# Linear attention, RMS norm and two MLPs on one core: q times kv in one float32 product, one function for the inverse root, and another model of time behind the order

## The chip, the cores and the metric

The kernel runs on one core of a Trainium2 chip. The time is the device time of one execution in microseconds (us). Runs of the kernel before gave 1581.61, 1582.32 and 1583.42 us; their median, 1582.32, is the time that the change is measured against. The engines of the core are named as in the profile: PE (TensorE, matmuls; PEld is its weight load), DVE (VectorE), ACT (ScalarE), POOL (GpSimd) and SP (SyncE, which here only issues DMAs). Each works through its own list of instructions in order.

## What is computed

Eight batches of eight heads with 576 rows of 64 go through linear attention without a softmax, each row is divided by its root mean square, and the result passes two MLPs whose weights are 512 x 2048 and 2048 x 512.

```python
kv = np.einsum('bhsd,bhse->bhde', k, v)
out = np.einsum('bhsd,bhde->bhse', q, kv)
rms = np.sqrt(np.mean(out * out, axis=-1, keepdims=True) + 1e-06)
x = (out / rms * g_norm)            # then heads side by side: x is 4608 x 512

h = x @ w_in                        # first MLP
g = np.where(h >= 1, h, np.where(h <= -1, 0.0, (h + 1) ** 2 / 4))
x = g @ w_out

h = x @ w_in2                       # second MLP
r = np.maximum(h, 0.0)
return (r * r) @ w_out2
```

## The kernel before

All inputs are float32. Nearly every product is made of three matmuls in a rounded 32-bit format: each operand is split into a high part (a cast, on ACT) and a remainder (a subtract, on DVE), and high x high, high x remainder and remainder x high are summed in one bank. `mm3` and `mm_group` issue such threes; in the profile they are L242 and L880. Tiles hold features across the 128 partitions and 512 of a batch's 576 rows along the free axis; the 64 rows that are left of each batch are gathered and go through at the end.

The work has two parts.

In the **blocks** (to about 540 us) the batches 0 to 4 of the first MLP run one after the other, 16 steps each. A step multiplies x by one 128-wide piece of w_in (`h_stage`, banks ph), forms u with two passes of ACT and one of DVE (L704, L228, L706), splits it (`g_stage`: cast L221 and subtract L234 into gs), and two steps later adds its product with w_out into four banks acc (`out_stage`). At the end of a block the four acc banks are evicted (ev) and stored to DRAM as x1d. Beside these steps stand: the attention of the next batch, the loads and splits of the weights (raw, d, j, w, s, wt), and their stores back to DRAM (wsd), from which the second part takes its weights as ws. Those stores are issued by ACT (`owe` and `pay`) or by SP.

In the **phases** (from about 523 us) two batches are multiplied together by a scheme with seven products in place of eight. Phase n has an input half (banks ph{n}, 336 matmuls) and an output half (banks po{n}, 336 matmuls); n runs from 0 to 6, and 6 is the narrow one with the rows left over. The attention of batches 5 to 7 is hosted inside phases 0 and 1.

The **attention** of a batch b goes over four pairs of heads hp, in this chain. `kv_stage` (L486 on PE, bank pkv) multiplies k and v of a pair, or of two pairs at once, and copies the two 64 x 64 blocks of each pair out of the bank, into kvbd, one of two tiles with zeros off its blocks: high part by an ACT cast (L221), remainder by DVE (L499). `t_stage` transposes q on DVE (L565) and splits it: cast by ACT (L221, qT0), remainder by DVE (L567, qT1). `o_stage`, once for each half of 288 rows, multiplies (three matmuls at L242, bank po), squares the bank twice on ACT (L588 rounded, L589 exact), scales it by g (L213) and, after the second half, takes the remainder of the squares on DVE (L594). `r_stage` sums the squares of each half over the head with a matrix of ones (L608, bank pr), takes the logarithm of each half (L609), one exponential over both halves (L611), squares that (L228), makes a Newton step for the inverse root with the banks pr (L526, L622 or L529) and multiplies by the scaled product. Its result is split into x (batches 1 to 4: L221, L234), or stored to DRAM (batches 5 to 7). The first two pairs of batch 1 (`WHOLE`) are not split: their q times kv is one float32 matmul for each half (L576). Batch 0 has its own short forms (`o_first`, `r_first`), all in float32. pkv, po and pr share the banks of one small pool, so a kv product of a later pair can be behind a pr whose bank has not been read out.

The **order** of all this is set in two layers. The code lists the stages by slots (`attention` and the hooks), and a scheduler then orders the instructions of every engine by priority and by a model of when each would be ready. An engine follows its list strictly. DMAs of SP and ACT take, in the scheduled order, one of eight lanes in turn, and a DMA starts its issue when the one that had the lane before it has landed; while ACT waits to issue a store, its further instructions wait too.

Of the kernel before, what the change touches and what calls it, by code (L numbers as in the profile page):

```python
# [16 lines left out]

LN_SCALE = 2.0**-44  # L20
LN2 = 0.6931471805599453


# [54 lines left out]
def linear_attention_rms_two_mlps(  # L78
# [115 lines left out]
    lnb = const.tile([P, 1], F32, name="lnb")  # L194
    expb = const.tile([P, 1], F32, name="expb")
# [3 lines left out]
    kvbd = [const.tile([P, 2, P], F32R, name=f"kvbd{i}") for i in range(2)]  # L199
# [274 lines left out]
    def kv_stage(*pairs):  # L474
# [12 lines left out]
        for n, (b, hp) in enumerate(pairs):  # L487
            for j in range(2):
                s = slice(j * D, (j + 1) * D)
                d = slice(n * P + j * D, n * P + (j + 1) * D)  # L490
                if b == 0:
                    copy(engine("kv_hi", b), kv0[s, hp, s], ps[s, d])
                    continue
                if (b, hp) in WHOLE:
                    copy(engine("kv_hi", b), kvw[s, hp % 2, s], ps[s, d])
                    continue
                t = kvbd[turn[b, hp] % len(kvbd)]
                copy(engine("kv_hi", b), t[s, 0, s], ps[s, d])
                nc.vector.tensor_tensor(t[s, 1, s], ps[s, d], t[s, 0, s].bitcast(F32), ALU.subtract)  # L499
# [34 lines left out]
    def r_first(hp):  # L534
# [3 lines left out]
        for half in range(2):  # L538
# [3 lines left out]
            nc.scalar.activation(y[:, half], m, AF.Ln, bias=lnb, scale=LN_SCALE)  # L542
# [13 lines left out]
    def t_stage(b, hp):  # L556
        work = [ap1.tile([P, S], F32, tag=f"wk{n}", name=f"wk{n}_{b}_{hp}") for n in range(2)]
        if (b, hp) in WHOLE:
            qT = ap1.tile([P, S], F32, tag="hl0", name=f"qT_{b}_{hp}")
            nc.vector.transpose(qT, qs.pop((b, hp)))  # L560
            hl[b, hp] = (work, qT)
            return
        qT = ap1.tile([P, S], F32, tag="wk2", name=f"qf_{b}_{hp}")
        parts = [ap1.tile([P, S], F32R, tag=f"hl{n}", name=f"qT{n}_{b}_{hp}") for n in range(2)]
        nc.vector.transpose(qT, qs.pop((b, hp)))  # L565
        copy(engine("q_hi", b), parts[0], qT)
        engine("q_lo", b).tensor_tensor(parts[1], qT, parts[0].bitcast(F32), ALU.subtract)  # L567
        hl[b, hp] = (work, parts)

    def o_stage(b, hp, half):  # L570
        work, parts = hl[b, hp]
        kv = kvbd[turn[b, hp] % len(kvbd)]
        c = slice(half * U, (half + 1) * U)
        if (b, hp) in WHOLE:
            ps = bank(b, f"po_{b}_{hp}_{half}")
            nc.tensor.matmul(  # L576
                ps[:, :U], kvw[:, hp % 2, :], parts[:, c], start=True, stop=True
            )
# [7 lines left out]
        ps = bank(b, f"po_{b}_{hp}_{half}")  # L586
        mm3(ps[:, :U], lambda a: kv[:, a, :], lambda a: parts[a][:, c], True, True)
# [8 lines left out]
    def r_stage(b, hp):  # L596
# [6 lines left out]
        for half in range(2):  # L603
# [5 lines left out]
            nc.scalar.activation(y[:, c], m, AF.Ln, bias=lnb, scale=LN_SCALE)  # L609
            ms.append((c, m))  # L610
        nc.scalar.activation(y, y, AF.Exp, bias=expb, scale=-0.5)  # L611
        pool, tag = (ap1, "wk2") if b < PLAIN else (ap2, "q")
        t = pool.tile([P, S], F32, tag=tag, name=f"t_{b}_{hp}")
        square(engine("y", b), t, y)
        for c, m in ms:
            newton(t[:, c], m)
        if b < PLAIN:
            norm(t, y, o)
# [3 lines left out]
        nc.vector.scalar_tensor_tensor(t, t, -3.0, y, op0=ALU.add, op1=ALU.mult)  # L622
        nc.vector.tensor_tensor(o, o, t, ALU.mult)
# [548 lines left out]
    nc.scalar.preload_act_table_set("natural_log_exp_and_others")  # L1172
# [18 lines left out]
    for t in kvbd:  # L1191
        nc.vector.memset(t.bitcast(F32), 0.0)
# [4 lines left out]
    nc.vector.memset(lnb, LN_SCALE * 1e-6)  # L1197
    nc.vector.memset(expb, -22.0 * LN2)
# [131 lines left out]
```

## Time and profile before

| | before |
|---|---|
| runs, median of 3 | 1582.32 us |
| profiled execution, its own time | 1577.18 us |
| its span in the profile | 1575.4 us |
| PE busy, 7633 matmul records | 1544.0 us (98%) |
| PE weight loads | 1268.9 us (81%) |
| DVE busy | 1195.8 us (76%) |
| ACT busy | 929.3 us (59%) |
| DMA | 388 MB, mean 246 GB/s |

How to read it: busy times are sums over the whole span, so they are averages over stages with different limits. Matmuls are pipelined and overlap in their records; a PE that is busy can still be slowed by what it is fed. The stage windows among the rows below have these columns: the window in us, its length, busy time with the count of instructions for PE, PEld, DVE, ACT and POOL, then the granted clock of PE as a share of 2.4 GHz, the share of the time in which the DMA engines were busy, and GB/s. The profiled execution took 1.78 us more than its span, and 5.14 us less than the median of the runs.

### The profile page before, as it was taken

The page shows a single profiled execution, that of the slowest core. Times are in us where ns is not written, and L with a number is a line of the kernel's source. Part 1 is how long each engine was busy: PE and PEld are TensorE (multiplying, and loading weights), DVE is VectorE, ACT ScalarE, POOL GpSimd, SP SyncE. Part 2 cuts the span into 40 slices and gives each one's busy share as a digit, 9 for nine tenths or more (in the row PEclk, how much of TensorE's full clock was granted, in tenths as well). Part 3 has the DMA queues.
Part 4 walks back from the last instruction along what each step waited for, and adds up shares of the span by engine and source line. Part 5 has one row for each costly group of instructions (what it writes and reads, how often), then busy time and mean ns, then how long its engine had stood idle before and what let it go on. Part 6 is the DMA issues. An engine that isn't in the chain of part 4 may idle for free.

```text
span 1575.4 us, 22379 instructions
## 1 busy us (share of the span) xinstructions
PE 1544.0 (98%) x7633; PEld 1268.9 (81%) x7633; DVE 1195.8 (76%) x2112; ACT 929.3 (59%) x1751; POOL 13.4 (1%) x30
## 2 busy tenths in 40 slices
PE   9999989999999999999989999999999999999999
PEld 5787768878877788787778888888888888888899
DVE  6975878786989678975689788868974597559666
ACT  5976666766756566735576466546653464446354
POOL 0000000000000000000000000000000000000000
PEclk9999999999999999999999999999999999999999
DMA  9676899796899966878767877776776676977797
GB/s 286 199 246 193 286 307 327 229 292 208 256 353 346 320 195 207 261 219 226 229 199 234 226 242 242 225 220 196 243 232 208 198 243 199 243 236 221 224 387 254
DMA packets 330914, 388.17 MB, mean 246 GB/s; under 512 B 197808, under 2 KB 223408, under 8 KB 330800
## 3 DMA queue, kind: packets, MB, share of 16 engines
q1 hardware_dynamic: 299904, 330.63, 69.2%
q10 hardware_dynamic: 30896, 56.11, 9.5%
q8 instruction: 61, 1.00, 0.3%
q14 instruction: 53, 0.43, 0.1%
HBM read 300.42 MB, written 86.25 MB: 245 GB/s over the span
## 4 chain that ended last, share of the span: by engine, by line
PE 84%; DVE 6%; ACT 5%; DMA 3%; issue 1%; SPq 0%; ACTq 0%; DVEq 0%
PE ph L880 32%; PE po L880 29%; PE acc L242 10%; PE ph L242 9%; PE pkv L486 1%; PE po L242 1%; PE pr L608 1%; DMA wsd<-s 1%; DVE s L189 1%; DVE u L706 1%; PE pwarm L1183 1%; DMA ws<-wsd 1%; DMA rest<-in_v_dram 0%; DVE t L809 0%; DMA wt<-wsd 0%
## 5 line engine op out<-in xcount | busy, mean ns | idle before, releaser
L880 PE MATMUL ph<-x,ws 128*128 128x512 f32 (+1 forms) x2352 | 507.1, 376 | 0.5 <-DVE e L936 0.5
L880 PEld LDWEIGHTS ph<-x,ws 128*128 128x128 f32 x2352 | 419.4, 189 | 79.5 <-DVE e L936 1.2
L880 PE MATMUL po<-t,ws 128*128 128x512 f32 x2016 | 461.7, 390 | 1.5 <-DMA ws<-wsd 0.8
L880 PEld LDWEIGHTS po<-t,ws 128*128 128x128 f32 x2016 | 377.1, 188 | 82.0 <-DVE t L809 3.3
L809 DVE TENSOR_TENSOR t<-g,t 128x512 fp32r<-128x512 f32 (+1 forms) x336 | 215.6, 647 | 84.1 <-ACT t L221 81.7
L221 ACT CAST t<-g 128x512 fp32r<-128x512 f32 (+1 forms) x336 | 195.5, 591 | 120.7 <-PE po L880 62.9
L242 PE MATMUL ph<-x,w 128*128 128x512 f32 x960 | 243.1, 396 | 7.6 <-DVE u L706 6.0
L242 PEld LDWEIGHTS ph<-x,w 128*128 128x128 f32 x960 | 177.4, 189 | 50.5 <-DVE u L706 10.5
L242 PE MATMUL acc<-gs,w 128*128 128x512 f32 x528 | 134.4, 398 | 3.5 <-DVE u L706 1.5
L957 ACT ACTIVATE g<-h 128x512 f32<-128x512 f32 (+1 forms) x120 | 70.4, 589 | 95.8 <-DVE h L946 95.8
L242 PEld LDWEIGHTS acc<-gs,w 128*128 128x128 f32 x528 | 98.6, 190 | 25.6 <-DVE u L706 2.0
L946 DVE CUSTOM_DVE_ANT_0 h<-ph,e 128x512 f32<-128x512 f32 (+1 forms) x120 | 76.1, 636 | 51.6 <-PE ph L880 47.6
L936 DVE TENSOR_TENSOR e<-ph,e 128x512 f32<-128x512 f32 (+1 forms) x112 | 72.1, 649 | 56.2 <-PE ph L880 47.8
L242 PE MATMUL acc<-gs,wt 128*128 128x512 f32 x432 | 106.5, 394 | 1.9 <-DVE gs L234 1.9
L242 PEld LDWEIGHTS acc<-gs,wt 128*128 128x128 f32 x432 | 81.8, 190 | 19.2 <-DVE gs L234 2.4
L221 ACT CAST x<-xr 128x512 fp32r<-128x512 f32 (+1 forms) x98 | 57.1, 590 | 41.7 <-DVE xr L860 23.5
L221 ACT CAST gs<-u 128x512 fp32r<-128x512 f32 x80 | 49.7, 622 | 47.4 <-DVE u L706 39.1
L706 DVE SCALAR_TENSOR_TENSOR u<-u,ph 128x512 f32<-128x512 f32 x80 | 54.4, 680 | 30.0 <-ACT u L228 29.9
L704 ACT ACTIVATE u<-ph,halfb 128x512 f32<-128x512 f32 x80 | 55.3, 691 | 24.7 <-PE ph L242 18.8
L234 DVE TENSOR_TENSOR gs<-u,gs 128x512 fp32r<-128x512 f32 x80 | 54.8, 686 | 17.1 <-ACT gs L221 16.6
L933 ACT COPY e<-ph 128x512 f32<-128x512 f32 (+1 forms) x56 | 30.8, 553 | 58.4 <-PE ph L880 51.5
L809 DVE TENSOR_TENSOR x<-xr,x 128x512 fp32r<-128x512 f32 (+1 forms) x98 | 62.6, 644 | 2.0 <-ACT x L221 1.9
(135 smaller groups left out, 1620.9 us busy)
## 6 DMA issues: line engine op xcount, KB each, us to landing
ws<-wsd SPq DMA_DIRECT2D x392, 512.0 KB, 4.4
wsd<-s ACTq DMA_DIRECT2D x96, 512.0 KB, 5.7
wt<-wsd SPq DMA_DIRECT2D x36, 512.0 KB, 5.5
raw<-in_moe_w_in_dram SPq DMA_DIRECT2D x32, 512.0 KB, 7.0
raw<-in_moe_w_out_dram SPq DMA_DIRECT2D x32, 512.0 KB, 6.1
xr<-x1d SPq DMA_DIRECT2D x36, 256.0 KB, 5.2
out_dram<-ov SPq DMA_DIRECT2D x142, 64.0 KB, 3.7
wsd<-w SPq DMA_DIRECT2D x17, 512.0 KB, 4.0
```

The lines of the kernel that those rows point to most:

```text
L189: lo.tensor_tensor(t[:, :, 1, :], src, t[:, :, 0, :].bitcast(F32), ALU.subtract)
L221: return e.copy(dst, src)
L234: lo = engine(op + "_lo", phase).tensor_tensor(t[:, 1, :], src, t[:, 0, :].bitcast(F32), ALU.subtract)
L242: nc.tensor.matmul(dst, wt(a), xt(c), start=first and n == 0, stop=last and n == 2)
L704: nc.scalar.activation(u, ps, AF.Relu, bias=halfb, scale=0.5)
L706: nc.vector.scalar_tensor_tensor(u, u, 1.0, ps, op0=ALU.min, op1=ALU.max)
L809: engine2(op + "_lo").tensor_tensor(t[:, 1, :], src, t[:, 0, :].bitcast(F32), ALU.subtract)
L880: nc.tensor.matmul(ps, wt(a), xt(c), start=first and n == 0 and i == 0, stop=last and n == len(lhs) - 1 and i == 2, skip_group_check=True,)
L933: nc.scalar.copy(e[i, 1], bank)
L936: nc.vector.tensor_tensor(e[i, p], bank, e[i, 1], ALU.add)
L946: nc.vector._custom_dve(TENSOR_ADD_SAT, out=h, in0=bank, in1=add, s0=float("inf"), s1=0.0)
L957: nc.scalar.activation(g, h, AF.Square)
```

## The change

Three things change. The context that schedules the program is given the option `schedule_with_timeline_sim=True`, so that the scheduler uses a finer model of time for each instruction. q times kv is one float32 matmul for each half in all batches from 1 on, so qT is not split, kvbd holds one float32 block matrix, and the four steps that made the parts go (26 casts and 26 subtracts for q, 52 subtracts for kv, and 104 matmuls). And the inverse root is one function of ACT for each half, `Abs_reciprocal_sqrt` with the bias 1e-6, in place of the logarithm for each half and the exponential over both; the scaled product o is multiplied by the root's estimate y beside the square, and the Newton step then ends in one operation. 32 activations go; DVE has as many operations there as before, in another order.

```diff
-    kvbd = [const.tile([P, 2, P], F32R, name=f"kvbd{i}") for i in range(2)]
+    kvbd = [const.tile([P, P], F32, name=f"kvbd{i}") for i in range(2)]
...
-                t = kvbd[turn[b, hp] % len(kvbd)]
-                copy(engine("kv_hi", b), t[s, 0, s], ps[s, d])
-                nc.vector.tensor_tensor(t[s, 1, s], ps[s, d], t[s, 0, s].bitcast(F32), ALU.subtract)
+                copy(engine("kv_hi", b), kvbd[turn[b, hp] % len(kvbd)][s, s], ps[s, d])
...
-    def norm(t, y, o):
-        nc.vector.scalar_tensor_tensor(t, t, -3.0, y, op0=ALU.add, op1=ALU.mult)
-        nc.vector.tensor_tensor(t, o, t, ALU.mult)
+    def norm(dst, t, o):
+        nc.vector.scalar_tensor_tensor(dst, t, -3.0, o, op0=ALU.add, op1=ALU.mult)
...
         if (b, hp) in WHOLE:
...
-        qT = ap1.tile([P, S], F32, tag="wk2", name=f"qf_{b}_{hp}")
-        parts = [ap1.tile([P, S], F32R, tag=f"hl{n}", name=f"qT{n}_{b}_{hp}") for n in range(2)]
+        qT = ap1.tile([P, S], F32, tag="hl0", name=f"qT_{b}_{hp}")
         nc.vector.transpose(qT, qs.pop((b, hp)))
-        copy(engine("q_hi", b), parts[0], qT)
-        engine("q_lo", b).tensor_tensor(parts[1], qT, parts[0].bitcast(F32), ALU.subtract)
-        hl[b, hp] = (work, parts)
+        hl[b, hp] = (work, qT)
...
+        ps = bank(b, f"po_{b}_{hp}_{half}")
+        nc.tensor.matmul(ps[:, :U], kv, qT[:, c], start=True, stop=True)
...
-        ps = bank(b, f"po_{b}_{hp}_{half}")
-        mm3(ps[:, :U], lambda a: kv[:, a, :], lambda a: parts[a][:, c], True, True)
...
-            nc.scalar.activation(y[:, c], m, AF.Ln, bias=lnb, scale=LN_SCALE)
+            nc.scalar.activation(y[:, c], m, AF.Abs_reciprocal_sqrt, bias=epsb)
             ms.append((c, m))
-        nc.scalar.activation(y, y, AF.Exp, bias=expb, scale=-0.5)
         pool, tag = (ap1, "wk2") if b < PLAIN else (ap2, "q")
         t = pool.tile([P, S], F32, tag=tag, name=f"t_{b}_{hp}")
         square(engine("y", b), t, y)
+        nc.vector.tensor_tensor(o, o, y, ALU.mult)
         for c, m in ms:
             newton(t[:, c], m)
         if b < PLAIN:
-            norm(t, y, o)
+            norm(t, t, o)
...
-        nc.vector.scalar_tensor_tensor(t, t, -3.0, y, op0=ALU.add, op1=ALU.mult)
-        nc.vector.tensor_tensor(o, o, t, ALU.mult)
+        norm(o, t, o)
...
-    nc.scalar.preload_act_table_set("natural_log_exp_and_others")
+    nc.scalar.preload_act_table_set("abs_reciprocal_sqrt_and_small")
...
-    nc.vector.memset(lnb, LN_SCALE * 1e-6)
-    nc.vector.memset(expb, -22.0 * LN2)
+    nc.vector.memset(epsb, 1e-6)
...
-    with _tile.TileContext(nc) as tc:
+    with _tile.TileContext(nc, schedule_with_timeline_sim=True) as tc:
```


The option moves instructions on all engines. Three places show how; in the names, ph1 and po1 are phase 1, pkv_7_0 is the kv product of pair 0 of batch 7, and the numbers at the ends count tiles. A suffix xN means N matmuls in a row.

On PE in phase 1, between the last pr of batch 6 and the first q times kv of batch 7, before:

```order
L608 MATMUL pr_6_3_0_7611<-s2_6_3_7503,ones_123 128x288
L608 MATMUL pr_6_3_0_7611<-s2lo_6_3_7540,ones_123 128x288
L880 MATMUL ph1_5_2_7513<-x2_1_3_0_6723,ws2_0_1_3_7455 128x512 x3
L880 MATMUL ph1_5_2_7513<-x2_1_3_1_6925,ws2_0_1_3_7455 128x512 x3
L880 MATMUL ph1_5_3_7523<-x2_1_3_0_6723,ws2_0_1_3_7455 128x512 x3
L880 MATMUL ph1_5_3_7523<-x2_1_3_1_6925,ws2_0_1_3_7455 128x512 x3
L608 MATMUL pr_6_3_1_7615<-s2_6_3_7503,ones_123 128x288
L608 MATMUL pr_6_3_1_7615<-s2lo_6_3_7540,ones_123 128x288
L242 MATMUL po_7_0_0_7710<-qT0_7_0_7631,kvbd0_131 128x288
```

After, with rows left out in the middle that are all of phase 1:

```order
L586 MATMUL pr_6_3_1_7362<-s2_6_3_7260,ones_123 128x288
L586 MATMUL pr_6_3_1_7362<-s2lo_6_3_7291,ones_123 128x288
L857 MATMUL ph1_6_5_7423<-x2_1_6_1_6650,ws2_0_2_6_7264 128x512
L857 MATMUL ph1_1_4_7386<-x2_1_2_0_6469,ws2_0_2_2_7293 128x512 x3
L857 MATMUL ph1_1_4_7386<-x2_1_2_1_6673,ws2_0_2_2_7293 128x512 x3
...
L857 MATMUL ph1_6_5_7423<-x2_1_7_0_6399,ws2_0_2_7_7338 128x512 x3
L857 MATMUL ph1_6_5_7423<-x2_1_7_1_6621,ws2_0_2_7_7338 128x512 x2
L557 MATMUL po_7_0_0_7451<-qT_7_0_7376,kvbd0_130 128x288
```

The product po_7_0_0, which stood directly behind pr_6_3_1, has moved behind 29 matmuls of phase 1, and is one matmul.

On PE a little later in phase 1, at the sums of squares of pair (7,1), before, with the two pr halves back to back:

```order
L608 MATMUL pr_7_1_0_7998<-s2_7_1_7893,ones_123 128x288
L608 MATMUL pr_7_1_0_7998<-s2lo_7_1_7928,ones_123 128x288
L608 MATMUL pr_7_1_1_8002<-s2_7_1_7893,ones_123 128x288
L608 MATMUL pr_7_1_1_8002<-s2lo_7_1_7928,ones_123 128x288
L880 MATMUL ph1_5_6_7978<-x2_1_5_0_6593,ws2_0_3_5_7851 128x512 x3
```

After, with rows of phase 1 left out:

```order
L586 MATMUL pr_7_1_0_7723<-s2_7_1_7628,ones_123 128x288
L586 MATMUL pr_7_1_0_7723<-s2lo_7_1_7657,ones_123 128x288
L857 MATMUL ph1_6_6_7609<-x2_1_4_0_6520,ws2_0_3_4_7607 128x512 x3
L857 MATMUL ph1_6_6_7609<-x2_1_4_1_6720,ws2_0_3_4_7607 128x512 x3
...
L857 MATMUL ph1_5_6_7703<-x2_1_3_1_6697,ws2_0_3_3_7632 128x512 x3
L586 MATMUL pr_7_1_1_7727<-s2_7_1_7628,ones_123 128x288
L586 MATMUL pr_7_1_1_7727<-s2lo_7_1_7657,ones_123 128x288
```

Between the two halves, whose banks come from the pool that pkv and po use too, 18 matmuls of phase 1 now stand.

On PE at the end of block 0, from the last pr of batch 1 to the first matmul on the x made from it (x1_1_3), before, with rows of blocks 0 and 1 left out:

```order
L608 MATMUL pr_1_3_1_1418<-s2_1_3_1323,ones_123 128x288
L608 MATMUL pr_1_3_1_1418<-s2lo_1_3_1354,ones_123 128x288
L242 MATMUL ph1_0_14_1432<-x1_0_2_221,w1_0_14_1087 128x512
L242 MATMUL ph1_0_14_1432<-x1_0_3_222,w1_0_14_1087 128x512 x3
...
L242 MATMUL acc1_0_0_850<-gs1_0_14_1450,w1_1_14_1302 128x512 x3
L242 MATMUL acc1_0_1_851<-gs1_0_14_1450,w1_1_14_1302 128x512 x3
L242 MATMUL ph1_1_0_1502<-x1_1_3_705,w1_0_0_302 128x512
```

After, without a gap:

```order
L586 MATMUL pr_1_3_0_1385<-s2lo_1_3_1325,ones_123 128x288
L586 MATMUL pr_1_3_1_1389<-s2lo_1_3_1325,ones_123 128x288
L234 MATMUL acc1_0_1_844<-gs1_0_15_1457,w1_1_15_1348 128x512 x3
L234 MATMUL acc1_0_2_845<-gs1_0_15_1457,w1_1_15_1348 128x512 x3
L234 MATMUL acc1_0_3_846<-gs1_0_15_1457,w1_1_15_1348 128x512 x3
L478 MATMUL pkv_2_0_1490<-v_2_0_1330,k_2_0_1327 64x64 x8
L478 MATMUL pkv_2_0_1490<-rest0_128 64x64 x2
L478 MATMUL pkv_2_0_1490<-v_2_1_1336,k_2_1_1333 64x64 x8
L234 MATMUL ph1_1_0_1472<-x1_1_3_699,w1_0_0_300 128x512
```

The first matmul on x1_1_3 stood 43 matmuls behind pr_1_3_1, and now stands behind nine of acc1_0 and a kv product of batch 2: the x that is read is made in a chain over ACT and DVE from that pr.

## Rows read from the trace of the kernel before

**Rows 1.** Stage windows; columns as named under the table of the profile above.

```profile
0.00:52.00 52.00, 48.60 (x277) 30.88 (x277) 38.92 (x88) 35.04 (x68) 3.67 (x14) 1.00 0.95 278
52.00:540.00 488.00, 474.91 (x2363) 382.38 (x2362) 386.86 (x724) 330.16 (x643) 9.69 (x16) 0.99 0.84 273
540.00:881.60 341.60, 330.30 (x1635) 270.84 (x1636) 264.88 (x441) 202.92 (x397) 0.00 (x0) 0.99 0.76 225
881.60:1491.20 609.60, 609.60 (x2690) 504.40 (x2690) 450.15 (x722) 319.55 (x536) 0.00 (x0) 1.00 0.74 224
```

**Rows 2.** Chain of waits, late links: start us, length us, what.

```profile
881.59 76.16 PE ph L880 x336
...
1531.47 40.33 PE po L880 x336
```

**Rows 3.** PE's waits in 52:540, then 540:882: total us, times, longest.

```profile
PE ph L242 <- DVE u L706: 6.0, 7, 2.5
...
PE po L242 <- ACT qT L221: 3.9, 1, 3.9
PE pr L608 <- DVE kvbd L499: 3.5, 1, 3.5
PE pr L608 <- ACT wk L213: 1.9, 2, 1.3
```

**Rows 4.** A window as in rows 1, and a link of the chain.

```profile
718.60:724.00 5.40, 5.40 (x21) 4.49 (x21) 3.49 (x7) 3.79 (x7) 0.00 (x0) 0.68 1.03 250
...
718.90 4.32 PE ph L880 x12
```

**Rows 5.** Instruction groups by form: busy us, mean ns | idle us before.

```profile
L609 ACT ACTIVATE wk<-pr,lnb 128x288 f32<-128x288 f32 x56 | 26.8, 504 | 15.7 <-PE pr L608 15.5
L526 DVE SCALAR_TENSOR_TENSOR t<-pr,t 128x288 f32<-128x288 f32 x64 | 26.6, 450 | 3.4 <-ACT t L228 3.2
...
L611 ACT ACTIVATE wk<-wk,expb 128x576 f32<-128x576 f32 x28 | 22.0, 784 | 0.3
...
L588 ACT ACTIVATE s<-po 128x288 fp32r<-128x288 f32 x52 | 21.6, 415 | 27.1 <-PE po L242 23.8 <-DVE d L274 2.9 <-issue 0.3
...
L567 DVE TENSOR_TENSOR qT<-qf,qT 128x576 fp32r<-128x576 f32 x26 | 19.6, 753 | 5.8 <-ACT qT L221 5.5
...
L228 ACT ACTIVATE t<-wk 128x576 f32<-128x576 f32 x28 | 19.2, 685 | 0.2
...
L221 ACT CAST qT<-qf 128x576 fp32r<-128x576 f32 x26 | 17.4, 669 | 7.9 <-DVE qf L565 7.6
...
L221 ACT CAST x<-t 128x512 fp32r<-128x512 f32 x20 | 12.3, 617 | 16.2 <-DVE t L530 16.1
...
L499 DVE TENSOR_TENSOR kvbd<-pkv,kvbd 64x64 fp32r<-64x64 f32 x52 | 11.4, 220 | 9.9 <-ACT kvbd L221 9.1
```

**Rows 6.** Chain links of a float32 and a split pair, then their groups.

```profile
65.33 0.97 PE po L576 x4
...
780.24 0.79 PE po L242 x6
...
L242 PE MATMUL po<-qT,kvbd 128*128 128x288 f32 x156 | 29.8, 304 | 5.3 <-ACT qT L221 4.1 <-DVE qT L567 1.1
...
L576 PE MATMUL po<-qT,kvw 128*128 128x288 f32 x8 | 2.3, 411 | 0.0
```

**Rows 7.** Timeline near 750: start, length, instruction, [idle before <- releaser].

```profile
751.04 0.66 ACT L221 CAST qT<-qf 128x576 fp32r<-128x576 f32 x1
...
751.80 0.67 PE L242 MATMUL po<-qT,kvbd 128*128 128x288 f32 x2 [3.89 <-ACT qT L221]
```

**Rows 8.** Timelines near 228 and 498, ACT and PE.

```profile
228.09 0.63 ACT L228 ACTIVATE u<-u 128x512 f32<-128x512 f32 x1 [4.83 <-DMA rest<-in_v_dram]
...
229.49 4.55 PE L242 MATMUL ph<-x,w 128*128 128x512 f32 x12 [2.50 <-DVE u L706]
...
498.52 0.69 ACT L704 ACTIVATE u<-ph,halfb 128x512 f32<-128x512 f32 x1 [4.04 <-DMA k<-in_k_dram]
```

More of the change, by code (lines that the diff above doesn't have):

```diff
@@ L541, in r_first @@
             nc.tensor.matmul(m, ones.bitcast(F32), y[:, half], start=True, stop=True)
-            nc.scalar.activation(y[:, half], m, AF.Ln, bias=lnb, scale=LN_SCALE)
+            nc.scalar.activation(y[:, half], m, AF.Abs_reciprocal_sqrt, bias=epsb)
             ms.append(m)
-        nc.scalar.activation(y, y, AF.Exp, bias=expb, scale=-0.5)
         square(engine("y", 0), t, y)
+        nc.vector.tensor_tensor(o, o, y, ALU.mult)
         for half in range(2):
             newton(t[:, half], ms[half])
-        norm(t, y, o)
+        norm(t, t, o)
         n = TB // 2
@@ L557, in t_stage @@
         work = [ap1.tile([P, S], F32, tag=f"wk{n}", name=f"wk{n}_{b}_{hp}") for n in range(2)]
[L558 to L562, printed above, removed]
-        qT = ap1.tile([P, S], F32, tag="wk2", name=f"qf_{b}_{hp}")
-        parts = [ap1.tile([P, S], F32R, tag=f"hl{n}", name=f"qT{n}_{b}_{hp}") for n in range(2)]
+        qT = ap1.tile([P, S], F32, tag="hl0", name=f"qT_{b}_{hp}")
         nc.vector.transpose(qT, qs.pop((b, hp)))
-        copy(engine("q_hi", b), parts[0], qT)
-        engine("q_lo", b).tensor_tensor(parts[1], qT, parts[0].bitcast(F32), ALU.subtract)
-        hl[b, hp] = (work, parts)
+        hl[b, hp] = (work, qT)
     def o_stage(b, hp, half):
-        work, parts = hl[b, hp]
-        kv = kvbd[turn[b, hp] % len(kvbd)]
+        work, qT = hl[b, hp]
+        whole = (b, hp) in WHOLE
+        kv = kvw[:, hp % 2, :] if whole else kvbd[turn[b, hp] % len(kvbd)]
         c = slice(half * U, (half + 1) * U)
-        if (b, hp) in WHOLE:
-            ps = bank(b, f"po_{b}_{hp}_{half}")
-            nc.tensor.matmul(
-                ps[:, :U], kvw[:, hp % 2, :], parts[:, c], start=True, stop=True
-            )
+        ps = bank(b, f"po_{b}_{hp}_{half}")
+        nc.tensor.matmul(ps[:, :U], kv, qT[:, c], start=True, stop=True)
+        if whole:
             nc.scalar.activation(work[0][:, c], ps[:, :U], AF.Square)
@@ L585, in o_stage @@
         s2 = og[b, hp]
-        ps = bank(b, f"po_{b}_{hp}_{half}")
-        mm3(ps[:, :U], lambda a: kv[:, a, :], lambda a: parts[a][:, c], True, True)
         nc.scalar.activation(s2[0][:, c], ps[:, :U], AF.Square)
@@ L614, in r_stage @@
         square(engine("y", b), t, y)
+        nc.vector.tensor_tensor(o, o, y, ALU.mult)
         for c, m in ms:
@@ L617, in r_stage @@
         if b < PLAIN:
-            norm(t, y, o)
+            norm(t, t, o)
             nc.gpsimd.tensor_copy(xrem[b][:, hp, :], t[:, TB:])
@@ L1191, in linear_attention_rms_two_mlps @@
     for t in kvbd:
-        nc.vector.memset(t.bitcast(F32), 0.0)
+        nc.vector.memset(t, 0.0)
     for t in rests:
```

6 lines of the change are left out of this document (1 added, 5 removed).

## The prediction

> **What bounds the kernel now.** I read the stage windows first [rows 1]. TensorE (PE) is busy in 1544.0 of 1575.4 us, and from 881.6 on its busy time equals the stage: 609.60 of 609.60. The chain of waits says the same of the end [rows 2]: from there every link is a block of 336 matmuls on PE (eight of about 76.16 us, two of 40.3), with nothing between. So the last 694 us hold work, not waits. They can move only if PE gets other work, and the change gives them none.
>
> What can be won lies before 881.6. PE's busy row makes it look small (3.4 + 13.1 + 11.3 = 28 us in three stages), but a matmul that trickles along at the pace of its neighbours counts as busy. The weight loads show better what is lost: in the waitless stage they fill 504.40/609.60 = 0.827 of the time, and at that ratio the loads of the three early stages would fill 37, 462 and 328 us, where 52, 488 and 341.6 passed [rows 1]. I therefore take 15, 26 and 14 us as lost, 55 in all. The Trainium skill's page "Perfetto Trace Analysis", section "Identifying the Most-Contended Engine", says likewise that matmul busy time tells little of headroom and weight-load busy time tells it; by the first the room is 28 us, by the second 55, and the waitless stage above is what decides it here.
>
> Then the waits of PE [rows 3]. In 52:540 they are small and many; the largest kind is DVE's u, 6.0 us in 7 pieces. In 540:882, where the attention of batches 5 to 7 runs inside phases 0 and 1, three kinds make 9.3 us: po on the rounded qT 3.9, pr on the kvbd remainder 3.5, pr on ACT's scaled copy 1.9. Behind such a wait PE runs slower for a while: in 718.60:724.00 the granted clock is 0.68, so between the levels 1.2 and 2.4 GHz, and 12 matmuls take 4.32 us [rows 4], where 12 take 12 x 76.16/336 = 2.72 in the waitless stage. I price this tail at 1.6 us for each wait of over a microsecond.
>
> **The change part by part.** *q times kv in float32.* For the 26 (batch, pair) products that were split, the rounding of q on ACT (26 x 669 ns = 17.4 us), its remainder on DVE (26 x 753 ns = 19.6) and the remainder of kv (52 x 220 ns = 11.4) go [rows 5]. Neither engine's sum sets the end: in 52:540 DVE is busy 386.86 and ACT 330.16 of 488 us [rows 1]. What counts is where these steps stand in the chain to po, below. On PE six matmuls become two. In the chain the six took 0.79 us; the two that were already float32 (four records, two for a product) took 0.97 [rows 6]: +0.18 x 26 = **+4.7 us**, on the bounding engine, uncovered. Bounds: by the busy time of the groups, 2.3 us for two pairs and 29.8 for 26, both cost 1.15 and the sum is 0; twice the chain's difference, were the overlap with the neighbours worse in the new places, gives +9.4. I keep to the chain, since it counts an overlap once. The Trainium skill's page "FP8 and Floating Point Precision", section "TensorE Precision Notes", gives float32 four passes; by four of the present passes of 0.132 us a pair would cost 1.05 us, the sum +6.9 instead of +4.7. The rows have the operation itself, so I keep 4.7.
>
> *Inverse root by one function.* The Ln of each half becomes a reciprocal root and the Exp over the pair goes: 32 x 784 ns = 25.1 us off ACT. The new function has no row. Bounds for 288 elements: the shortest 288-wide read of a bank on ACT in this trace's groups, 0.415 us, and twice the Ln, 1.01; I take Ln's 0.504 [rows 5], the same engine, shape and bias. Even at 1.01 it adds 0.5 us to a chain that loses 0.78. The multiply by o moves from behind the Newton step to beside the square; the count on DVE stays, the chain loses another 0.75. So pr to x is 1.5 us shorter. In the start that chain is run through once with nothing beside it: **-1 us**, between 0 and -3.
>
> *The order.* With the finer model all engines' instructions are put in another order, not only those that the diff names. I follow three places.
>
> First, the pair (7,0) in phase 1. Before, po_7_0 stands right behind the second pr of (6,3), and waits 3.89 us for the cast of qT, which itself stands behind Exp and square on ACT [rows 7]. After, 29 matmuls, at 76.16/336 = 0.227 us each 6.6 us, lie between, and the cast is gone. Second, the pair (7,1): before, the two halves of pr_7_1 stand back to back and the second waits 3.5 us [rows 3] for a bank, which four rounds of copy and subtract between ACT and DVE hold. After, 18 matmuls (4.1 us) lie between, and the subtracts are gone. The same holds behind nearly every po of later blocks: before, the next pr followed with 0 to 1.6 us of cover at seven of them, after with 5 or more. So these waits go (9.3 [rows 3]) and two tails of 1.6 with them: -12.5; I leave 1.1 for new ones: **-11.4** for the hosted stretch, bounds -14 and -5 (the lower if only the removed steps help).
>
> Third, the end of block 0, which becomes worse. Before, 43 matmuls (9.7 us) stand between the last pr of batch 1 and the first matmul that needs its x; after, 9 matmuls and a kv product, about 3 us. The chain to x costs 0.504 (root) + 0.685 (square) + 0.90 (two Newton halves) + 0.75 (one more pass of DVE, the length of its other 576-wide passes) + 0.617 (cast) [rows 5] = 3.5 us when nothing is queued ahead of it. But on ACT now the four evictions of block 0 and their DMA issues stand there, on DVE the preparation of weights. I price it at +7 (a wait of some 5 and a tail), bounds +2 and +10. PE is in order, so every matmul of block 1 waits with it.
>
> For the rest of 52:540, some 26 us lost, I split by what ended the waits. ACT was held twice by its own store, which waited for a DMA: 4.83 us before the square of u at 228.09 and 4.04 at 498.52 [rows 8]; after the first PE waited 2.50 us and then took 4.55 us over 12 matmuls. The order can move these, but DMA lanes are shared round-robin between SP and ACT before and after, so I leave them and a late weight load, 9 us. Of the other 17 nearly all comes from narrow covers, which the new order widens (matmuls that had under 3 us of other PE work ahead since their last input go from 32 to 5), so -16; with the boundary's +7: **-9**.
>
> Last, in the out phases from 881.6 on the order now takes the high products of both halves before the low ones and pulls groups of the next phase ahead. Nothing waited there, so this can only lose: **+1.5**, bounds 0 and +5.
>
> Sum: +4.7 - 1 - 11.4 - 9 + 1.5 = -15.2. Against the profiled execution: 1577.2 - 15.2 = 1562.0. That execution lay 5.1 us under the median of the runs; so **1567.0** for the median.
>
> **The rivals.** *Larger gain:* the boundary costs nothing, because ACT's queue is empty when pr lands, the holds by the DMA vanish with the new order of the loads, and the start gains its 3. Then 52:540 wins 20 (26 less a third of the 17 that come from covers): -20 - 12.5 - 3 + 4.7 = -30.8, so 1551.5. For it speaks that the weight loads show 55 us lost; against it, the narrow cover of 3 us at the boundary.
>
> *The order brings nothing:* a model that counts more finely can still be wrong on this chip, and then only the removed steps act: the hosted waits shrink by 5 with a tail of 2, small qT waits by 1.5, the start by 1.5, against +4.7: -5.3, so 1577. For it: a model can't know when a DMA lands.
>
> *No change:* that case, and the boundary takes its +7: 1584, within 0.2% (3.2 us) of 1582.3, which is about what a measurement of this kernel tells apart.
>
> *Slower:* a store on ACT's own queue is held by the DMA lane it is given, and everything behind it on ACT, u included, waits. Each of the two holds in the trace costs PE 2.5 plus a tail of 2 or so, about 4.7 us [rows 8]. In the new order the loads of the attention come in bunches behind rows of stores, so ACT's stores may meet more lanes that are full. From four more such holds (+18.8) the gain is gone; with five the time is 1590.5. Against it: of ACT's DMAs those whose lane was last used by a load or store of SP fall from 86 to 80.
>
> **How the numbers follow.** My forecast 0.43 (1558 to 1574 about it), larger gain 0.19, the order brings nothing 0.11, no change 0.10, slower 0.17. Faster is the first three, 0.73. The range takes the forecast, the two next cases and most of no change, the larger gain down to 1549 and the slower one's beginning, to 1588; about 0.08 is left out at the lower and 0.1 at the upper end.
>
> **What would show it.** In the changed profile: float32 po pairs of 0.97 us in the chain; no wait of PE over 1 us in the hosted stretch, and weight loads in 0.81 or more of its time; a wait of the first ph matmuls of block 1 near 130 us on DVE's or ACT's x; no PE gap in the phases from then on. I am wrong if PE waits for ACT's u behind DMA releases more than twice, if the wait at the boundary repeats at each block, or if the late phases show gaps.

## The result and the profile after

The changed kernel took 1600.21 us (median of 5 runs, 1592.43 to 1601.18), the kernel before, on the same chip, 1581.61: a ratio of 1.0105, 95% interval 1.0076 to 1.0133. A second set of runs (changed_again) gave 1599.74 against 1578.30, 1.0140 (1.0125 to 1.0155). Forecast was 1567, with a range from 1549 to 1588. The profiled execution took 1594.92 us with a span of 1593.1, 17.7 us more than the span before. Two single executions, one of before_sp (2608.91 us) and one of the kernel before (3810.57 us), are left out of the ratios below.

The stage windows of the changed kernel, columns as in [rows 1]:

```profile
52.00:540.00 488.00, 473.75 (x2339) 382.53 (x2337) 369.57 (x681) 316.43 (x621) 17.60 (x16) 1.00 0.86 275
540.00:881.60 341.60, 328.74 (x1588) 266.44 (x1587) 246.29 (x398) 185.23 (x364) 0.00 (x0) 0.99 0.80 221
881.60:1491.20 609.60, 602.84 (x2639) 493.54 (x2638) 442.85 (x714) 308.12 (x528) 0.00 (x0) 1.00 0.74 220
```

In the last of these windows, where before PE was busy all of the time and its weight loads filled 504.40 us [rows 1], PE now stands idle for 6.8 us and the weight loads fill 493.54. At the old ratio of 0.827 the missing 10.9 us of loads are 13 us of time. The stretch in fact lost about 11 (table below). So the weight loads name the loss better than PE's busy time, as the Trainium skill's "Perfetto Trace Analysis", section "Identifying the Most-Contended Engine", has it.

The chain of waits (start, length, what) of the changed kernel holds one long link for the input half of each of phases 3 to 5:

```profile
1045.57 70.27 PE ph L857 x310
...
1202.20 70.27 PE ph L857 x310
...
1356.78 70.27 PE ph L857 x310
```

From one to the next are 156.6 and 154.6 us; before, a phase took 609.6/4 = 152.4 [rows 1]. PE's waits (total, times, longest), in 52:540, then 540:882, then 882:1593:

```profile
PE ph L234 <- DVE u L683: 5.0, 3, 2.4
PE po L557 <- ACT kvbd L213: 3.1, 1, 3.1
PE acc L234 <- ACT gs L213: 2.8, 1, 2.8
...
PE pr L586 <- ACT wk L205: 8.5, 4, 2.5
...
PE po L857 <- DVE t L786: 4.3, 8, 0.8
PE po L857 <- ACT t L213: 1.8, 3, 1.3
```

The first group answers to the 6.0 us on u and the small ones of [rows 3]. In the second the waits on qT and kvbd of [rows 3] are gone, and the one on ACT's scaled copy (L213 before, L205 now) has grown from 1.9 to 8.5. The third has no row before: PE waits for t, the split input of the output halves.

Where the time goes stage by stage is best seen by the work done. I numbered the 6624 wide matmuls of the MLPs by their start in each trace, and took how much later (+) or earlier (-) than in the kernel before the same number starts. One column is the changed kernel; the kernels of the other five are explained below.

```
matmul  place (us before)           changed  no_order  order_only  x_behind_t_late  x_behind_t_store  stores_on_sp
  768   in block 1 (244)               -7.7      +3.8        +4.0             -6.1              -5.8          -4.0
 1536   in block 4 (437)               -3.4      +4.9       +40.1             +1.5              -0.9          -4.0
 1920   end of the blocks (533)        +0.5      +7.6       +48.9             +4.8              +2.4          -9.4
 2256   input half of phase 0 (619)    +2.8      +7.0       +47.8             +7.1              +4.7          -7.9
 2592   end of phase 0 (700)          +12.0      +6.0       +56.2            +16.4              +9.0          -2.8
 2928   input half of phase 1 (801)    +0.5      +6.5       +45.9             +6.2              -4.1         -13.1
 3264   end of phase 1 (881)           +5.9      +5.0       +52.0            +13.8              -2.8         -11.1
 5280   end of phase 4 (1339)         +17.5      +5.2       +64.4            +14.6              -0.9          -9.7
 6288   end of phase 6's input (1531) +17.6      +5.2       +64.4            +14.9              -0.8          -9.4
```

One execution each, so a difference of 4 or 5 us at one place means little: the changed kernel's second execution (changed_again), the same program, is 4.2 us later than its first at 1536 and 8.0 later in the last row. The first was among its faster ones (1594.92 us, median 1600.21), so x_behind_t_late ends only 2.7 us below it here. What repeats is the pattern: in the changed kernel the input half of phase 1 wins 11.5 us, the output halves of phases 0 and 1 lose 9.2 and 5.4, and those of phases 2, 3 and 4 lose 4.4, 4.3 and 2.3; in changed_again it wins 11.3, and they lose 9.8, 7.6, 4.7, 4.2 and 2.0.

### The profile page after: what moved, and what is told of

Read it like the earlier page. It is cut to its first block, busy times and chain, and to the rows that moved or that the text cites. A ratio compares the mean times of both kernels' runs of the same rounds, so it can differ in the third digit from the quotient of the medians.

```text
span 1593.1 us, 22201 instructions
## 1 busy us (share of the span) xinstructions
PE 1551.0 (97%) x7581; PEld 1267.8 (80%) x7581; DVE 1161.3 (73%) x2033; ACT 890.9 (56%) x1693; POOL 20.9 (1%) x30
## 4 chain that ended last, share of the span: by engine, by line
PE 73%; DVE 11%; DMA 10%; ACT 3%; issue 2%; SPq 1%; ACTq 0%; DVEq 0%
PE ph L857 29%; PE po L857 24%; PE acc L234 8%; PE ph L234 8%; DVE t L786 2%; DMA raw<-in_moe_w_in_dram 2%; DMA xr<-x1d 2%; DVE x L786 1%; PE pkv L478 1%; PE po L557 1%; DMA xrd<-wk 1%; PE pr L586 1%; DMA xr<-xpd 1%; DVE xr L837 1%; DVE s L182 1%
## 5 line engine op out<-in xcount | busy, mean ns | idle before, releaser
L857 PE MATMUL po<-t,ws 128*128 128x512 f32 x2016 | 472.8, 393 | 6.4 <-DVE t L786 4.3
L857 PEld LDWEIGHTS po<-t,ws 128*128 128x128 f32 x2016 | 378.3, 189 | 91.8 <-DVE t L786 10.9
L213 ACT CAST t<-g 128x512 fp32r<-128x512 f32 (+1 forms) x336 | 196.1, 592 | 128.8 <-PE po L857 67.4
L213 ACT CAST x<-xr 128x512 fp32r<-128x512 f32 (+1 forms) x98 | 56.4, 591 | 28.3 <-DMA xr<-x1d 18.6
L213 ACT CAST gs<-u 128x512 fp32r<-128x512 f32 x80 | 49.8, 624 | 33.3 <-DVE u L683 22.2
```

Source lines behind the costliest of these rows:

```text
L213: return e.copy(dst, src)
L857: nc.tensor.matmul(ps, wt(a), xt(c), start=first and n == 0 and i == 0, stop=last and n == len(lhs) - 1 and i == 2, skip_group_check=True,)
```

## The experiments

Ratios are to the kernel before, run beside each, with 95% intervals.

### Which part of the change loses: four kernels

order_only is the kernel before with the option alone, no_order the changed kernel without it:

```diff
-    with _tile.TileContext(nc) as tc:
+    with _tile.TileContext(nc, schedule_with_timeline_sim=True) as tc:
```

> The kernel before with only the scheduler's option. Theory O (the new order loses what the changed one lost, the removed steps gain): slower than before by 20 to 30 us, 1602 to 1612, with PE waits in the output halves of phases 0 to 4 as in the changed kernel. Rival P (the new forms of product and root lose, the order is neutral): 1578 to 1585. Rival I (each alone gains, only together they lose): 1565 to 1578.

1642.81 us, 1.0407 (1.0390 to 1.0425).

> The changed kernel without the scheduler's option: float32 product and one-function root in the old order. Theory O: faster than before by 4 to 12 us, 1570 to 1578, no PE wait after 882 us. Rival P: 1595 to 1602, like the changed kernel. Rival I: 1570 to 1578 as well; order_only tells it from O.

1579.92 us, 1.0004 (0.9992 to 1.0017).

f32_only takes from the change the float32 product (kvbd, `t_stage`, `o_stage`), root_only the inverse root (`norm`, `r_first`, `r_stage`), both in the old order.

> The kernel before with only q times kv in float32. Theory O: the three hosted waits of 9.3 us shrink by 6 to 9 with their tails, the float32 product takes 4.7 back: 1575 to 1580. Rival P: 1590 or more.

1577.39 us, 0.9991 (0.9979 to 1.0002).

> The kernel before with only the inverse root by one function and the early multiply. Theory O: 25 us less on ACT, nearly all beside PE's work: 1577 to 1582. Rival P (the new function is much slower than the logarithm, 1 us or more for 288 columns): 1585 or more, seen in its duration.

1580.46 us, 1.0010 (0.9996 to 1.0024).

So the whole loss is the order's, and in the old order the removed steps gain nothing, though 42 us of ACT and 31 of DVE went. PE's waits of no_order in 540:890 show why:

```profile
PE po L557 <- DVE qT L548: 3.4, 1, 3.4
PE po L557 <- DVE t L516: 2.5, 1, 2.5
PE pr L586 <- ACT kvbd L213: 1.8, 2, 0.9
PE pr L586 <- ACT wk L205: 1.8, 2, 1.2
```

They sum to 9.5 us, as much as the 9.3 of [rows 3]: where the casts and subtracts are gone, the transpose of q (L548) and the Newton step that still reads a shared bank (L516) are late in their place. The option alone costs 64 us, 31 more than theory O allowed and 43 more than with the other parts. Its PE waits in 52:600:

```profile
PE ph L242 <- ACT x L221: 17.8, 4, 9.2
PE pkv L486 <- DVE t L526: 15.9, 3, 6.9
```

These stand at the ends of blocks, where x of the next batch is made late: that is the third place of the prediction, four times over. In the changed kernel they are 1.6 and 0.6 us. Its chain to x is shorter by the exponential and one pass of DVE; whether that is the reason was not tried apart.

### Where the order loses: a cut, and the option on one side of it

The kernel is cut into two scheduled parts where phase 2 begins. cut_only has no option, early_fine has it up to the cut, fine_cut on both sides.

```diff
+    early = tc.block(schedule_with_timeline_sim=True)
+    early.__enter__()
     nc.scalar.preload_act_table_set("abs_reciprocal_sqrt_and_small")
...
         if n == max(HOSTED) + 1:
+            early.__exit__(None, None, None)
```

> The changed kernel without the option, cut into two scheduled parts where phase 2 begins. Prices the cut: against the changed kernel without option (1579.9) the drain and refill of PE, 2 to 6 us: 1582 to 1586.

1580.51 us, 1.0012 (1.0002 to 1.0022): the cut itself is nearly free.

> The changed kernel with the option for the part up to the end of phase 1 only, cut there; its instructions stand up to the cut as in the changed kernel. Theory L (the order of the late phases loses 11 us, by letting DVE's work for the next phase's x stand ahead of the t that PE needs): 11 us less than fine_cut, 1588 to 1592, no PE wait after the cut. Rival C (the late waits are a consequence of what the hosted phases leave late): within 3 us of fine_cut. Theory E beside both: against cut_only it loses 5 to 8 us, all in the output halves of phases 0 and 1.

1589.40 us, 1.0047 (1.0028 to 1.0067).

> The changed kernel with the same cut and the option in both parts; up to the cut the same order as early_fine. Theory L: 1599 to 1605, the changed kernel and the price of the cut, with PE waits for DVE's t in phases 2 to 4. Rival C: within 3 us of early_fine.

1606.11 us, 1.0162 (1.0143 to 1.0182). In the hosted phases the two traces lose alike (6.1 and 5.8 us), and behind the cut early_fine has no PE wait, fine_cut 5.7 us in 11 on DVE's t. But of the 16.7 us between them some belong to fine_cut's cut, where PE waited for the first weights of phase 2:

```profile
PE ph L857 <- DMA ws<-wsd: 4.6, 1, 4.6
```

By the count of matmuls fine_cut lost 7.6 us there and 11.7 in phases 2 to 4, early_fine none and 1.4. So the late order costs some 10 us, and the early one about 9 (1589.4 against 1580.5).

### Which engine's order: one engine held to the order of the code

From phase 2 on one engine issues in the order of the code, the others as the option has it.

```diff
         if n == max(HOSTED) + 1:
+            fixed = tc.manual_schedule(engines={mybir.EngineType.PE})
+            fixed.__enter__()
```

> The changed kernel, but from phase 2 on PE issues its instructions in the order of the code; DVE, ACT and SP stay with the scheduler and its finer model, and DVE still takes the next phase's x early. Theory P (what loses the 11 us is PE's own order: groups of the output half pulled ahead and both halves' high products first, so that t tiles are held longer and are needed sooner): no PE wait after 890, 9 to 12 us less than the changed kernel. Theory D (DVE takes x ahead of the t that PE waits for): the waits stay, under 3 us less.

1601.03 us, 1.0145 (1.0125 to 1.0165), with changed_again beside it at 1599.74. PE's waits from 890 on:

```profile
PE po L857 <- DVE t L786: 8.1, 10, 1.8
```

PE's waits for t stay, against theory P. A PE tied to the code among engines that are not can make waits of its own, so this run alone doesn't price PE's order; x_behind_t_late below does more.

> The changed kernel, but from phase 2 on DVE issues its instructions in the order of the code, which spreads the x work evenly between the t; PE stays with the finer model. Theory D: no PE wait after 890 and 9 to 12 us less than the changed kernel. Theory P: the waits stay, under 3 us less, or more waits, since DVE now can't follow PE's order.

1689.54 us, 1.0704 (1.0687 to 1.0722).

> The changed kernel, but from phase 2 on ACT alone issues in the order of the code. Theory A (ACT's casts of x stand ahead of its casts of t): 9 to 12 us less. Theories P and D: under 3 us less.

1630.70 us, 1.0324 (1.0306 to 1.0343).

> The changed kernel once more, beside the three others, on the same chip: 1594 to 1602; its trace shows which of its waits come back in another execution. All theories expect PE waits for t in the output halves of phases 2 to 4, 10 to 12 us between the starts of phases 2 and 5.

1599.74 us. The runs on DVE and ACT decide nothing, whatever theory D expected of the first: an engine tied to the code while its neighbours follow another order makes all wait. Here are late_dve's waits of PE from 890 on:

```profile
PE po L857 <- DVE t L786: 40.5, 5, 15.1
PE ph L857 <- DVE e L913: 23.0, 6, 4.6
```

### The work for the next phase's x

In the output half of a phase DVE makes t, PE's next input, and beside it the split x of the next phase (remainders X, differences r). The order of DVE there, from the last work of the input half (h, g) through the first evictions f of product 6, phase 2, each letter one operation, up to the second f:

```
before           ...hghghghghggtgggtgtgtgtgtXtrXtXtrtrXtXtrtggtff
changed          ...hhgtggthhhgghtgXgrtgggtrXXgtXtXtXggttrrtttrXtXgXgtff
x_behind_t_late  ...hhgtggthhhgghtggtgggtgttggttXtrtrtXtgXrtgtff
```

Before the first f, DVE did 5 X and 4 r before, and does 9 and 5 in the changed kernel. In phases 0 and 1 it is 6 and 7 before, 18 now; in phase 4, 11 and 16; in phase 5, 20 and 22. By phase that is 12, 11, 5, 5, 5 and 2 operations more, and the output halves lost 9.2, 5.4, 4.4, 4.3, 2.3 and nothing. For phases 0 and 1 this is no proof: PE's waits there, 8.5 us, are for ACT's scaled copy, and none is for t. How it looks in phase 2, just behind the two f, DVE and PE of the changed kernel:

```profile
994.23 0.70 DVE L786 TENSOR_TENSOR x<-xr,x 128x512 fp32r<-128x512 f32 x1
...
994.83 0.70 DVE L977 TENSOR_TENSOR g<-g,g 128x512 f32<-128x512 f32 x1
995.43 0.70 DVE L786 TENSOR_TENSOR x<-xr,x 128x512 fp32r<-128x512 f32 x1
...
996.03 1.30 DVE L786 TENSOR_TENSOR t<-g,t 128x512 fp32r<-128x512 f32 x2
...
996.78 1.43 PE L857 MATMUL po<-t,ws 128*128 128x512 f32 x5 [0.78 <-DVE t L786]
```

Two remainders of x and a difference g stand before the t that PE waits for. DVE is all but full there in each order (29.08, 30.00 and 28.42 of 30 us); the windows of 30 us at that place, before, changed, and with x behind t:

```profile
970.00:1000.00 30.00, 30.00 (x134) 24.82 (x134) 29.08 (x49) 17.78 (x32) 0.00 (x0) 1.00 0.74 229
```

```profile
975.00:1005.00 30.00, 27.57 (x115) 20.85 (x114) 30.00 (x51) 20.19 (x37) 0.00 (x0) 1.00 0.70 220
```

```profile
975.00:1005.00 30.00, 30.00 (x133) 24.78 (x133) 28.42 (x48) 20.47 (x38) 0.00 (x0) 1.00 0.80 252
```

The edit makes DVE issue the x work of a step no earlier than the t that the code prepares in the same step:

```diff
-                jobs.pop(0)()
+                with tc.issue_after(behind[0]) if n >= 2 else ExitStack():
+                    jobs.pop(0)()
```

Here `behind[0]` is the subtract that makes the remainder of the latest t.

> The changed kernel, where from phase 2 on DVE issues what it does for the next phase's x (4 of 16 jobs at a time) no earlier than the t that the code prepares in the same step; nothing else is tied. Up to the first sum of product 6 DVE then has 3 remainders and 3 differences for x, not 9 and 5. Theory D (x work ahead of t makes PE wait): no PE wait for t after 890, the 11 us between the starts of phases 2 and 5 go, 1587 to 1591. Rival R (DVE simply has more work there than PE's time, whatever its order): the waits move to later products of the same half, under 4 us less than the changed kernel.

1589.62 us, 1.0055 (1.0034 to 1.0075), 10 us less than the changed kernel. PE's waits for t from 890 on:

```profile
PE po L860 <- DVE t L786: 0.3, 1, 0.3
```

By the count of matmuls phases 2 to 4 lose 0.8 us in place of 11.6. The late loss is the order of x and t on DVE. (PE's own order changed a little too, since the scheduler follows; with PE alone put back, in late_pe, nothing was won.)

> The same tie in all phases, the hosted ones too. Theory D: the 9 and 5 us that the output halves of phases 0 and 1 lose go for the most part as well, 1576 to 1583. Rival S (the hosted loss is the store that ACT's scaling waits for, as the waits of 8.5 us on it say): 1586 to 1591, like the one tied only from phase 2 on, with PE still waiting for ACT's scaled copy.

x_behind_t drops the condition `n >= 2`. 1583.54 us, 1.0026 (1.0014 to 1.0039), 6 us less again. But it wasn't won as theory D has it. With the late tie alone PE waits in 540:890 for the scaled copy and not for DVE's t:

```profile
PE pr L586 <- ACT wk L205: 9.4, 4, 2.5
```

With the tie in all phases this wait is down to 0.2 us, and PE waits 4.1 us for t (rows in the next section). By the count of matmuls, in one execution, the output halves of phases 0 and 1 still lose 7.5 and 2.7 us. About 2.7 us of the 7.5 is work that has moved: 40 of the 120 kv matmuls (pkv) that stood in the input half of phase 1 before stand in phase 0's output half now, and 14 in the changed kernel. So the tie gives 6 us in the hosted phases, but that x ahead of t is what lost them there isn't shown.

### The store that ACT's scaled copy waits for

ACT's copy L205 writes the tile from which the pair before is stored. In the changed kernel, SP, ACT and PE in phase 0:

```profile
644.50 7.23 SPq L773 DMA_DIRECT2D ws<-wsd  x3
651.83 0.38 SPq L601 DMA_DIRECT2D xpd<-wk  x1
...
657.42 0.89 ACT L205 ACTIVATE wk<-po,gvec 128x288 f32<-128x288 f32 x2 [3.10 <-DMA xrd<-wk]
...
657.97 0.61 PE L586 MATMUL pr<-s,ones 128*128 128x288 f32 x1 [2.51 <-ACT wk L205]
```

SP stands 7.23 us at three loads of weights that wait for PE to free their tiles; the two stores come behind them; ACT's copy of the next pair waits 3.10 us for them to land, and PE 2.51 for ACT. The edit stores from t, so that nothing waits for the store:

```diff
-        norm(o, t, o)
-        nc.sync.dma_start(xpd[b][:, hp, :], o[:, :TB])
-        nc.sync.dma_start(xrd[:, hp, b, :], o[:, TB:])
+        norm(t, t, o)
+        nc.sync.dma_start(xpd[b][:, hp, :], t[:, :TB])
+        nc.sync.dma_start(xrd[:, hp, b, :], t[:, TB:])
```

> The changed kernel, where batches 5 to 7 store the normalized pair from t instead of from the tile of the scaled product, so that ACT's scaling of the next pair needs no store to have landed. Theory W (the 8.5 us of PE waits for that scaling in the hosted phases come from the store, which stands on SP behind weight loads that wait for PE): the waits go with their tails, 8 to 13 us less than the changed kernel, 1586 to 1592. Rival A (ACT is late for other reasons; the store only came last): under 3 us less, 1597 to 1600, with PE still waiting for ACT at the same pairs.

1596.47 us, 1.0092 (1.0070 to 1.0114). The wait went as foretold, but the time fell by 3.7 us only against 1600.21, and its interval overlaps that of the changed kernel's first set, not that of the second; PE then waited in 540:890 for t:

```profile
PE po L857 <- DVE t L786: 5.5, 6, 1.4
...
PE pr L586 <- ACT wk L205: 0.8, 1, 0.8
```

> The tie in all phases, and batches 5 to 7 stored from t. If both S and D hold in part: 1572 to 1580, 3 to 8 us under the one with the tie alone. If the store only came last: within 3 us of it.

With x behind t as well: 1577.16 us, 0.9989 (0.9977 to 1.0001), 6.4 less than with x behind t alone. In x_behind_t, without the store's edit, PE's wait for the copy was down to 0.2 us in the profiled execution:

```profile
PE po L860 <- DVE t L786: 4.1, 3, 1.7
...
PE pr L586 <- ACT wk L205: 0.2, 1, 0.2
```

so that the 6.4 us are measured, but not seen as that wait. ACT itself still stands 14.3 us at those stores in 540:890 of x_behind_t, as it does 13.6 in the changed kernel. The 6.4 us do lie in the hosted phases: from matmul 1920 to 3264 x_behind_t falls 1.0 us further behind, and x_behind_t_store gains 5.3.

> Control: both edits (x work behind t, store from t) on the changed kernel without the option, in the old order, where x was not early and the store not late. Theory D expects within 3 us of no_order, 1577 to 1582: the edits repair what the option did and are no gain of their own. If they are a gain in themselves (then x_behind_t_store says nothing about the cause): 1570 or less.

1586.47 us, 1.0037 (1.0017 to 1.0057). In the old order both edits cost 6.5 us against no_order, more than the 3 that theory D allowed: they repair what the option's order did and are no gain of their own.

### The stores that ACT itself waits to issue

In block 4 of the changed kernel ACT stands still for 7 us; its queue and PE near 460 us:

```profile
459.93 0.37 ACTq L174 DMA_DIRECT2D wsd<-s  x1
460.34 0.62 ACT L213 CAST gs<-u 128x512 fp32r<-128x512 f32 x1 [6.99 <-DMA xr<-x1d]
...
461.01 1.23 PE L234 MATMUL acc<-gs,w 128*128 128x512 f32 x3 [2.83 <-ACT gs L213]
```

The store on ACT's queue waits for a load of xr that has the lane before it; SP began to issue that load at 450.1, and it landed just before the store starts, at 459.9. gs, behind the store, comes late, and PE with it. It is the longest of several such holds of ACT in 52:540:

```profile
ACT gs L213 <- DMA xr<-x1d: 7.0, 1, 7.0
...
ACT u L220 <- DMA x1d<-ev: 4.5, 2, 2.7
...
ACT u L220 <- DMA wsd<-s: 4.2, 1, 4.2
```

With both edits in place x_behind_t_store still waits so; PE in 52:540:

```profile
PE acc L234 <- ACT gs L213: 3.9, 1, 3.9
PE ph L234 <- DVE u L683: 3.5, 2, 2.0
```

The next kernel issues these stores by SP:

```diff
-                nc.scalar.dma_start(dst, src)
+                nc.sync.dma_start(dst, src)
```

> The changed kernel with both edits, and the 115 or so stores that ACT issued in the blocks issued by SP, so that ACT never waits for a DMA's place. Theory H (ACT held by its own store, once 7.3 us and several times 2 to 5, is what is left of the loss before 540): PE's waits there for gs, u and x fall by 6 to 9 us, 1567 to 1573. Rival Q (SP then stands still in ACT's place, and loads come late): 1578 to 1595, with PE waits for weights or for v and k.

1564.99 us, 0.9915 (0.9898 to 0.9932): faster than both kernels, and 2 us under what theory H expected. From matmul 768 to 1920 it gains 5.4 us, where x_behind_t_store loses 8.3. PE's longest waits in 52:540 are now:

```profile
PE po L557 <- ACT kvbd L213: 3.0, 1, 3.0
PE ph L234 <- ACT x L213: 1.8, 2, 1.2
```

> The kernel before with only ACT's stores of the blocks issued by SP. Theory H for the old order (two holds of 4.8 and 4.0 us on ACT, about 4.7 us of PE each): 1567 to 1573. If what the stores on SP gave is the option's order alone (its loads meet ACT's stores oftener): 1576 to 1581. Rival Q (SP late with loads): over 1582.

The same edit on the kernel before: 1631.18 us (median of three), 1.0323 (1.0302 to 1.0344). SP's waits in 52:600 for the remainder that it is to store, stores_on_sp first, then before_sp:

```profile
SPq L174 <- DVE s L182: 33.2, 28, 3.3
```

```profile
SPq L181 <- DVE s L189: 141.7, 31, 19.8
```

In the old order SP waits 141.7 us at stores whose data DVE hasn't finished, with the loads behind them; in the finer order it waits 33.2 us in 28. So this gain needs the new order. How SP's standing still reaches PE is argued, not shown: PE's longest waits of before_sp are for results of ACT and DVE, not for loads.

## Why the prediction was wrong

**The float32 product** was sized right. The chain of the changed kernel again has a pair at 0.97 us:

```profile
106.31 0.97 PE po L557 x4
```

That is +4.7 us for 26; an estimate from the Trainium skill's four passes ("FP8 and Floating Point Precision", "TensorE Precision Notes") gave 1.05 for a pair, and the chain has 0.97. In 14 of the 26 pairs the halves stand apart; there the starts of the wide matmuls around a half show 0.51 us for it, so 1.03 for a pair, against 0.81 in the split form. The sum over all pairs is then about +5.

**The inverse root.** The new function takes what the logarithm took, 504 ns [rows 5]; the group of the changed kernel:

```profile
L587 ACT ACTIVATE wk<-pr,epsb 128x288 f32<-128x288 f32 x56 | 26.6, 505 | 15.5 <-PE pr L586 12.4 <-DVE d L267 1.4 <-ACT g L934 0.5
```

The start gained 0.4 to 1.7 us by the count of matmuls, as foretold.

**The hosted stretch, -11.4, measured +5.4** (from matmul 1920 to 3264; 2.2 of it is the float32 product of its 12 pairs). The first step held: the places that I followed lie in the input half of phase 1, and it won 11.5 us. The step that failed is the sentence that the same holds elsewhere. I had counted covers in PE's list; the output halves of phases 0 and 1 lost 14.6 us, and PE waited there for ACT's scaled copy, which waited for stores that stood behind weight loads on SP. With both edits, the tie of x and the store from t, they lose 5.5. The shares of the two can't be told apart: with the store's edit alone PE waits for t instead (5.5 us), and the tie alone takes away the wait for the copy too. Nor did the removed steps carry the gain, as the rival that the order brings nothing assumed: no_order has as much wait there as before.

**52:540, -9, measured about +2.** The boundary has the size that I gave it, +7 with bounds 2 and 10: by the count of matmuls it cost 6.8 us (from matmul 396 to 408). Its waits on PE are these, 4.2 us in brackets:

```profile
136.66 0.69 PE L478 MATMUL pkv<-v,k 128*64 128x64 f32 x16 [0.55 <-DVE t L516]
...
138.54 1.93 PE L234 MATMUL ph<-x,w 128*128 128x512 f32 x6 [0.62 <-ACT x L213]
...
143.79 0.75 PE L557 MATMUL po<-qT,kvbd 128*128 128x288 f32 x2 [3.05 <-ACT kvbd L213]
```

That is partly luck: the wait for x, priced at some 5 us, is 0.62, and the longest, 3.05, is for the kv blocks of batch 2, which I didn't price. What failed is that the -16 from wider covers would last. Block 1 did win 13.4 us behind the boundary (5.7 late at matmul 528, 7.7 early at 768), and the hold at 228 [rows 8] is gone. Blocks 2 to 4 lost 8.2 of it again, to smaller waits and to ACT's stores, which held it longest at 460, for 7 us. I had left the holds of before in the sum, as if the new order kept their number and size; it took the two away and made others, longer in all.

**The late phases, +1.5 with bounds 0 and +5, measured +11.6.** In us the hosted stretch missed by more, but here the runs show the cause best, and the order of the lists would have shown it. I read PE's rows there, saw the high products first and groups pulled ahead, and priced those; with PE alone put back (late_pe) nothing was won, and with x put behind t on DVE 10 us were. "Nothing waited there" was true, but DVE was 97% busy in that place before, 29.08 of 30 us, and what it does first decides. The bound of +5 had no row behind it.

**The rivals.** The slower case was the right side with the wrong mechanism in first place. ACT held by its own store did occur, and taking all such stores off ACT gave 12 us. But of the 23 us that the first two edits gave back 16 came with the tie of x behind t, 10 of them in the late phases, and 6 with the store of the hosted pairs, and neither mechanism was on my list. Of my signs of being wrong the gaps in the late phases came. The chance of 0.17 for slower was too low: most of the forecast gain hung on an order that I had checked on one engine.

**What stays open.** Why the finer model takes x so early isn't settled; only that it does, and what it costs. The 6.4 us of the store beside x_behind_t were measured without a wait in the trace that shows them. x_behind_t still waits 4.1 us for t in phases 0 and 1. And after each edit the scheduler orders the rest anew, so what an edit gave includes what moved with it.

## What to carry to other kernels

When a change lets a scheduler reorder everything, compare the lists of the engines that feed the one that ends last, the fullest of them first (here DVE, busy for 29 to 30 of 30 us in its place), and look for work without haste that has moved ahead of work that PE waits for. Tie that work with an issue-order edge to the step that it must not overtake: one line gave 10 us back, and in all phases 16. Steps taken off engines that aren't the bound are worth what the next-late input leaves; here that was nothing, 9.5 us of waits for 9.3. And a store issued by a computing engine stops that engine when its DMA lane is taken. Issued by a queue that computes nothing, the stores cost 12 us less here, but 52 us more in an order where they stood on that queue waiting for unfinished data.

## What the runs showed of the hardware

- The reciprocal root on ACT takes 505 ns for 128x288, the logarithm 504 [rows 5].
- A pair of float32 products of 288 columns takes 0.97 us of PE in its chain, in old and new places alike, and 1.03 where the halves stand apart; the three-matmul form takes 0.79 [rows 6].
- A DMA that ACT issues can hold ACT: 6.99 us before one store, until the load that had its lane had landed.
- Two executions of the same program can differ by 4.2 us by 437 us into the kernel and by 8.0 at its end (-3.4 and +0.8, then +17.6 and +25.6 against before, changed and changed_again).
